# Weight splits through a PSUM copy, earlier keys for the second attention unit, and left output tiles finished ahead of right ones

## The chip, the core and the metric

The kernel runs on one core of a Trainium2 chip. A core has engines that each work through their own list of instructions in order: TensorE (PE in the profile, with PEld for its weight loads), VectorE (DVE), ScalarE (ACT), GpSimd (POOL), and SyncE (SP), whose list here holds DMA issues alone. They wait for each other through semaphores. An instruction that waits holds up all that stands behind it on the same engine. The metric is the device time of one execution in microseconds (us).

## What is computed

Two branches over the same input x of 2048 rows and 448 columns, mixed by a gate, all in float32:

```
g   = sigmoid((x * gate_w).sum(-1))
# A: 16 heads of 28, each row looks at 8 rows back at a stride of 2
q, k, v = split_heads(x @ wqkv)
idx     = pos[:, None] - 2 * arange(8)[None, :]
a       = softmax(where(idx >= 0, q . k[idx] / sqrt(28), -1e9)) . v[idx]   @ wo
# B: squared ReLU
b   = relu(x @ w1 + b1) ** 2 @ w2 + b2
out = g * a + (1 - g) * b
```

w1 is 448 x 1792, w2 is 1792 x 448, wo is 448 x 448.

## The kernel before

Every matmul operand is held as two parts: a rounded high part and the rest (low part). A product is three matmuls: high by high, high by low, low by high. A split is a copy on ACT that rounds (`split_full`, L115) and a subtraction on DVE that gives the rest (L116). K = 448 is three blocks of 128 and one of 64; two products of 64 rows are laid side by side on the upper and lower half of TensorE (`side_by_side`, L184), so one matmul pair takes the time of one. The halves swap after some pairs. Before a swap, a tiny write orders the new half behind the old: a memset on DVE into the accumulator (`turn`, L194), or a one-column ACT copy (`touch`, L516).

The rows are cut in four chunks of 512, each chunk in four tiles of 128 rows. There are two stages on TensorE.

**Stage A** makes q, k and v. Chunks 1 to 3 take two calls of `qkv_two` each, with 63 matmul pairs per call and six accumulators in PSUM banks of the two tags "m" and "b" (four banks each). ACT empties an accumulator into a staging tile (`qkv_evacuate`, L203, and L211 for the gate's column), SP stores it to DRAM (L209). The turns of a call stand after pairs 24, 33 and 42. Beside that, w1 (four pieces, `w1_piece`) and the first seven row blocks of w2 (two pieces, `w2_piece`) are loaded and split. All raw weights pass through a pool of two buffers, so a load waits until an earlier piece was read. In the last call the first MLP matmuls are laid between (`mlp_one` at pair 51, `mlp_two` at pair 57).

**Stage B** is the MLP, in the order of chunks 3, 0, 1, 2, with 7 steps per chunk. A step takes two blocks of 128 hidden columns: `h_first`, 12 matmul pairs; then `o_part(..., False)`, the first half of the output matmuls of the step before, for its left tiles (0, 1) and its right tiles (2, 3), 6 pairs each; `h_second`, 9 pairs; then `o_all(..., True)`, the second half of those output matmuls, 6 pairs left and 6 right. The result of h is squared on ACT (L565 to L567) and its low part made on DVE (L564), one for each of the two blocks; I call these two subtractions the first and the second h low. The next step's output matmuls need them. In the last step of a chunk the output accumulators are complete; `fin_add` (L751, DVE) scales them into a tile that SP stores. This falls in the first step of the next chunk, called the seam here. Its last lines before the change:

```
for tls in (left, right)[:1 if ends else 2]:
    o_part(pc, pf, False, tls)
o_turn(pc, pf, left if ends else both)
...
h_second(x, accs, f)
...
o_all(pc, pf, True)
```

**Attention** runs beside both stages, in 8 units (two halves of the rows by four groups of heads). POOL multiplies (L325 for q by k, L332 for weights by v), DVE sums (L326, L340), eight pieces per unit and product. POOL's products lie in four buffers, so POOL is at most four pieces ahead of DVE. After the fourth unit of a half, DVE transposes the sums in place (L342) and SP stores them; they come back for the matmuls with wo (`wo_first`, `wo_second`, tile "a").

**Who sets the order.** The kernel is recorded with a modelled TensorE clock: `advance(dt)` adds the estimated time of matmuls, and whatever is due by then is put on its engine's list: deferred work by `at(dt, ...)` and `when(t, ...)`, attention by the costs QK_COST, AV_COST, SM_COST and the waits ATT_DELAY (before the first unit) and KEY_DELAY (before the second). So constants in modelled nanoseconds decide where a subtraction stands between the sums on DVE, and where a load stands on SP. They decide no start times: these follow from the lists and the waits.

Of the kernel before, what the change touches and what calls it, by code (L numbers as in the profile page):

```python
# [14 lines left out]
P = 128  # L15
# [17 lines left out]
QK_COST = 2300.0  # L33
AV_COST = 2000.0
SM_COST = 600.0
ATT_DELAY = 20000.0
LO_DELAY = 1500.0
HL_DELAY = 1800.0
SPLIT_GAP = 2000.0
W2_GAP = 1500.0  # L40
ROW_GAP = 9200.0
OUT_DELAY = 2500.0
WO_DELAY = 4500.0
LOAD_DELAY = 1500.0
LAND_DELAY = 5000.0
OL_DELAY = 2500.0
KEY_DELAY = 10500.0
DEFER = 2
ORDER = (3, 0, 1, 2)
WARM = 13  # L50
# [7 lines left out]
def gated_mix_kernel(ctx: ExitStack, tc: tile.TileContext, xT, wqkv, w1, w2, wo, b1, b2, out):  # L58
# [169 lines left out]
    def accs(c, b, tls, tags):  # L228
        return [Acc(t, f"qkv{c}_{tl}_{b}", ncols(b)) for t, tl in zip(tags, tls)]

    def run(c, todo, steps):


        a = 0
        for e, done, *turns in steps:
            side_by_side(todo[0][a:e], todo[1][a:e])
            while a < e:
                advance(min(12, e - a) * MM448)
                a = min(a + 12, e)
# [30 lines left out]
            [(15, [], (v[0], v[1])), (24, [], (v[2], v[3])),  # L270
             (33, [(2, 0, v[0]), (2, 1, v[1])]), (42, [(2, 2, v[2]), (2, 3, v[3])])])

    def qkv_two(x, c, t0, beside=()):

        t1 = t0 + 1
        kinds = ("mm", "bm", "bb") if beside else ("mm", "mb", "bb")
        (q0, q1), (k0, k1), (v0, v1) = (accs(c, b, (t0, t1), tags) for b, tags in enumerate(kinds))
        run(c, [full(x, q0, t0, 0) + last(x, q0, t0, 0) + full(x, q1, t1, 0) + last(x, q1, t1, 0) + full(x, k0, t0, 1)
                + full(x, k1, t1, 1) + full(x, v0, t0, 2) + last(x, v0, t0, 2) + full(x, v1, t1, 2),
                full(x, k1, t1, 1) + last(x, k1, t1, 1) + full(x, v0, t0, 2) + full(x, v1, t1, 2) + last(x, v1, t1, 2)  # L280
                + full(x, q0, t0, 0) + full(x, q1, t1, 0) + full(x, k0, t0, 1) + last(x, k0, t0, 1)],
            [(24, [], (q0, k1)), (33, [], (q1, v0)), (42, [(0, t0, q0), (1, t1, k1)], (k0, v1)),
             (51, [(0, t1, q1)]), (51, [], *beside[:1]), (54, [(2, t0, v0)]), (57, [], *beside[1:]),
             (63, [(1, t0, k0), (2, t1, v1)])])
# [44 lines left out]
    def av_piece(u, par, g, v, lg, s):  # L329

        pr = prodp.tile([P, C, W], F32, tag="pp", name=f"av{u}_{s}", bufs=PP_BUFS)
        nc.gpsimd.tensor_mul(  # L332
            pr.rearrange("p (h d) w -> p w h d", h=HG),
            lg[:, s][:, :, :, None].to_broadcast([P, W, HG, DH]),
            v[:, s:s + W].rearrange("p w (h d) -> p w h d", h=HG),
        )
        o = o_t[par, s]

        def rest():
            nc.vector.tensor_reduce(o[:, g * C:(g + 1) * C], pr, axis=AX.X, op=ALU.add)  # L340
            if g == G - 1:
                nc.vector.transpose(o, o)  # L342
                at(OUT_DELAY, lambda: o_store(par, s))
        pending.append(rest)

    def o_store(par, s):
        nc.sync.dma_start(o_d[par, s], o_t.pop((par, s)))
        at(WO_DELAY, lambda: (wo_q.append((par, s)), wo_loads()))
# [102 lines left out]
    def at(dt, fn):  # L451

        later.append((clock["pe"] + dt, fn))
# [3 lines left out]

    def advance(dt):
        clock["pe"] += dt
        for item in sorted([x for x in later if x[0] <= clock["pe"]], key=lambda x: x[0]):  # L460
            later.remove(item)
            item[1]()
        if not clock["on"]:
            clock["att"] = clock["pe"]
            return
        while clock["att"] < clock["pe"]:
            try:
                r = next(att)
            except StopIteration:
                clock["on"] = False  # L470
                return
            if r is None:
                clock["att"] = clock["pe"]
                return
            clock["att"] += r
# [2 lines left out]
    def raw_tile(name):  # L478
        return rawp.tile([P, 4, 512], F32, tag="raw", name=name)

    def w1_piece(i, dt):

        n = F // 4
        raw = raw_tile(f"w1raw{i}")
        nc.sync.dma_start(raw[:, :, :n], w1[i])
        sl = slice(i * n, (i + 1) * n)

        def part(k):
            if k < 3:
                split_full(raw[:, k, :n], w1h[:, k, sl], w1l[:, k, sl], soon)  # L490
                return
            for a in range(i * n, i * n + n, 64):
                f, b = divmod(a, P)
                if b and a > i * n:
                    continue
                m = min(P - b, i * n + n - a)
                rows, o = slice(f % 2 * 64, f % 2 * 64 + 64), f // 2 * P + b
                split_full(raw[rows, 3, a - i * n:a - i * n + m], w17h[rows, o:o + m], w17l[rows, o:o + m], soon)
        for k in range(4):
            at(dt + k * SPLIT_GAP, lambda k=k: part(k))  # L500

    def w2_piece(i0, n, dt):
        raw = raw_tile(f"w2raw{i0}")
        nc.sync.dma_start(raw[:, :n, :D], w2[:, i0:i0 + n])
        for k in range(n):
            at(dt + k * W2_GAP, lambda k=k: split_full(raw[:, k, :D], w2ah[:, i0 + k], w2al[:, i0 + k], soon))

    def x_load(c):
        raw = raw_tile(f"xraw{c}")
# [138 lines left out]
            when(t + 4500.0, x_more, c + 1)  # L648
            when(t + 5000.0, lambda c: x_spill(c, xs[c]), c)
    when(10500.0, x_spill, 0, x)  # L650
    when(25000.0, w1_piece, 0, 13000.0)
    when(44500.0, halos)
    when(46500.0, w1_piece, 1, 12500.0)
    when(67000.0, w1_piece, 2, 10500.0)
    when(68000.0, w1_piece, 3, 15500.0)
    when(70000.0, biases)
    when(86000.0, w2_piece, 0, 4, 6500.0)
    when(91300.0, w2_piece, 4, 3, 6000.0)

    pair = {}  # L660

# [13 lines left out]
    for c in range(4):  # L675
        x = xs[c]
        if c == 0:
            qkv_first(x)
        else:
            qkv_two(x, c, 0)  # L680
            qkv_two(x, c, 2, (mlp_one, mlp_two) if c == 3 else ())
        if c == 1:
            st_["spilled"] = 0
            clock["on"] = True
            clock["att"] = clock["pe"] - 1.0
            advance(0.0)
        if c == 3:
            st_["spilled"] = 1
# [266 lines left out]
    for g in range(2, 2 * NF):  # L955
        i, f = g // (NF // 2), g % (NF // 2) * 2
        c = ORDER[i]
        pc, pf = (c, f - 2) if f else (ORDER[i - 1], NF - 2)
        ends = f == NF - 2 and i < 3
        last = g == 2 * NF - 1  # L960
        if not f:
            x, slots = X([nxt[j][0] for j in range(4)]), [nxt[j][1] for j in range(4)]
            nxt = {}
        accs = h_first(x, c, f)
        if f == 2 and 0 < i < 3:
            x_reload(i + 1, 3, free)
# [12 lines left out]
        if g == 2:  # L979
            o_all(c, 0, True)  # L980
            del hs[c, 0], hs[c, 1]
        for tls in (left, right)[:1 if ends else 2]:
            o_part(pc, pf, False, tls)
        o_turn(pc, pf, left if ends else both)
        if f in (NF - 6, NF - 4):
            for tl in left if f == NF - 6 else right:
                fin_prep(c // 2, (c % 2) * 4 + tl)
        h_second(x, accs, f)
        ops = mlp_ops(accs, c, f, (HL_DELAY, HL_DELAY if ends else 2 * HL_DELAY))
        emit(ops[:3])  # L990
# [12 lines left out]
        o_all(pc, pf, True)  # L1003
        del hs[pc, pf], hs[pc, pf + 1]
        if st:
            wo_second(st)
# [55 lines left out]
```

## Time and profile before

| | us |
|---|---|
| median of 3 runs | 423.88 |
| lowest and highest | 421.41, 424.59 |
| the profiled execution | 423.65 |
| its span, first to last instruction | 421.9 |
| TensorE busy in the span | 412.3 |
| POOL, DVE, ACT busy | 268.9, 260.9, 199.5 |

The profile is one execution; each time in it is counted from the start of its span. The time of an execution is 1.75 us longer than its span. A busy TensorE is not one at its peak, so idle time, and stretches in which fewer matmuls start, tell more than the share.

### The profile page before, as it was taken

How to read it: one execution, taken by the hardware profiler on the slowest of the kernel's cores; microseconds unless marked ns; L12 is line 12 of the kernel's file. 1: busy time of each engine (PE TensorE's matmuls, PEld its weight loads, DVE VectorE, ACT ScalarE, POOL GpSimd, SP SyncE). 2: the span in 40 equal slices, each digit the busy share in tenths (PEclk: the TensorE clock that was granted, in tenths of full speed). 3: DMA queues.
4: the chain of work that ended last, by engine and by line, in shares of the span. 5: the costliest groups of instructions: out<-in, count | busy, mean ns of one | idle time of the engine just before them, and what ended most of it. 6: DMA issues, size and time to landing. Idle time of an engine off the chain costs nothing.

```text
span 421.9 us, 9322 instructions
## 1 busy us (share of the span) xinstructions
PE 412.3 (98%) x3844; PEld 375.0 (89%) x3844; DVE 260.9 (62%) x403; ACT 199.5 (47%) x453; POOL 268.9 (64%) x167
## 2 busy tenths in 40 slices
PE   8999999999999999999999997999999999999995
PEld 8999999999799888888888886889998888888994
DVE  5420522384775776775776796798677577687343
ACT  4542555344566565445565342625552344346630
POOL 0000000950599999999898997799799879692000
PEclk9999999999999999999999998999999999999999
DMA  7999899938464053463220637882446320228804
GB/s 234 345 335 328 240 376 291 365 99 280 173 204 172 0 203 116 184 214 110 89 84 2 246 139 207 212 252 81 94 169 228 137 89 2 82 89 176 174 2 175
DMA packets 65322, 73.75 MB, mean 175 GB/s; under 512 B 32320, under 2 KB 58368, under 8 KB 64896
## 3 DMA queue, kind: packets, MB, share of 16 engines
q1 hardware_dynamic: 65280, 73.16, 52.9%
q8 instruction: 30, 0.49, 0.5%
q14 instruction: 12, 0.10, 0.1%
HBM read 45.71 MB, written 28.25 MB: 175 GB/s over the span
## 4 chain that ended last, share of the span: by engine, by line
PE 90%; DMA 3%; DVE 2%; POOL 2%; ACT 1%; SPq 0%; issue 0%; DVEq 0%; ACTq 0%
PE h L184 30%; PE b L184 29%; PE qkv L184 20%; PE a L184 8%; DMA w2raw<-w 3%; PE qkv L253 2%; POOL av L332 1%; DVE bt L751 1%; PE warm L576 1%; DVE o L340 1%; POOL w2bl L892 1%; DVE h L564 0%; SPq L710 0%; ACT st L203 0%; ACT w17h L115 0%
## 5 line engine op out<-in xcount | busy, mean ns | idle before, releaser
L325 POOL TENSOR_TENSOR qk<-q,k 128x896 f32<-128x896 f32 x64 | 135.9, 2156 | 104.2 <-DMA k<-k_d 89.3
L332 POOL TENSOR_TENSOR av<-lg,v 128x896 f32<-128x896 f32 x64 | 119.0, 1973 | 7.0 <-DMA v<-v_d 3.9
L184 PE MATMUL qkv<-wqh,x 64*128 64x448 f32 (+1 forms) x528 | 91.0, 362 | 0.0
L564 DVE TENSOR_TENSOR h<-h,h 128x512 fp32r<-128x512 f32 x56 | 38.6, 688 | 61.1 <-ACT h L567 60.8
L184 PE MATMUL qkv<-wql,x 64*128 64x448 f32 (+1 forms) x264 | 75.0, 362 | 0.0
L184 PEld LDWEIGHTS qkv<-wqh,x 64*128 64x128 f32 x528 | 74.0, 185 | 0.4
L184 PE MATMUL b<-w2ah,h 64*128 64x448 f32 x448 | 68.8, 364 | 2.5 <-DVE h L564 2.5
L326 DVE TENSOR_REDUCE lg<-qk 128x32 f32<-128x896 f32 x64 | 67.6, 1077 | 2.4 <-POOL qk L325 2.3
L340 DVE TENSOR_REDUCE o<-av 128x112 f32<-128x896 f32 x64 | 67.1, 1071 | 3.1 <-POOL av L332 2.9
L184 PE MATMUL b<-w2bh,h 64*128 64x448 f32 x448 | 66.6, 360 | 0.0
L565 ACT ACTIVATE h<-h,b1z 128x512 f32<-128x512 f32 x56 | 36.6, 654 | 41.0 <-PE h L184 41.0
L184 PEld LDWEIGHTS b<-w2ah,h 64*128 64x128 f32 x448 | 45.8, 186 | 6.8 <-DVE h L564 3.6
L184 PEld LDWEIGHTS b<-w2bh,h 64*128 64x128 f32 x448 | 41.9, 184 | 3.8 <-ACT h L516 0.3
L184 PEld LDWEIGHTS qkv<-wql,x 64*128 64x128 f32 x264 | 44.8, 185 | 0.2
L184 PE MATMUL b<-w2al,h 64*128 64x448 f32 x224 | 44.7, 362 | 0.0
L203 ACT ACTIVATE st<-qkv 128x448 f32<-128x448 f32 x48 | 24.6, 543 | 40.8 <-PE qkv L184 34.3
L184 PE MATMUL b<-w2bl,h 64*128 64x448 f32 x224 | 40.5, 359 | 0.0
L566 ACT ACTIVATE h<-h 128x512 fp32r<-128x512 f32 x56 | 33.5, 598 | 1.7
L567 ACT ACTIVATE h<-h 128x512 f32<-128x512 f32 x56 | 33.3, 594 | 0.0
L184 PE MATMUL h<-x,w1h 64*128 64x512 f32 x168 | 31.2, 387 | 0.0
L516 ACT ACTIVATE h<-h 128x4 fp32r<-128x4 f32 (+1 forms) x32 | 6.6, 207 | 47.0 <-PE b L184 46.9
L184 PE MATMUL h<-x1b,w1h 64*128 64x512 f32 x168 | 28.8, 395 | 0.0
(124 smaller groups left out, 718.0 us busy)
## 6 DMA issues: line engine op xcount, KB each, us to landing
k<-k_d SPq DMA_DIRECT2D x8, 840.0 KB, 5.3
v<-v_d SPq DMA_DIRECT2D x8, 840.0 KB, 4.7
x_d<-x SPq DMA_DIRECT2D x12, 512.0 KB, 5.2
q_d<-st SPq DMA_DIRECT2D x8, 448.0 KB, 6.5
k_d<-st SPq DMA_DIRECT2D x8, 448.0 KB, 5.6
v_d<-st SPq DMA_DIRECT2D x8, 448.0 KB, 7.4
w1raw<-w SPq DMA_DIRECT2D x4, 896.0 KB, 9.7
q<-q_d SPq DMA_DIRECT2D x8, 448.0 KB, 3.3
```

Source lines behind the costliest of these rows:

```text
L184: nc.tensor.matmul(acc.pt[:, :acc.n], a[rows], w[rows], start=acc.todo == acc.all, stop=acc.todo == 1)
L203: nc.scalar.activation(st[:, :, t % 2], pt[:, :D].rearrange("p (g c) -> p g c", g=G), AF.Copy)
L253: nc.tensor.matmul(acc.pt[:, :NQ], a, w, start=k == j == 0, stop=False)
L325: nc.gpsimd.tensor_mul(pr, q[:, s:s + 1].to_broadcast([P, W, C]), k[:, s:s + W])
L326: pending.append(lambda: nc.vector.tensor_reduce(lg[:, s], pr.rearrange("p w (h d) -> p w h d", h=HG), axis=AX.X, op=ALU.add))
L332: nc.gpsimd.tensor_mul(pr.rearrange("p (h d) w -> p w h d", h=HG), lg[:, s][:, :, :, None].to_broadcast([P, W, HG, DH]), v[:, s:s + W].rea ...
L340: nc.vector.tensor_reduce(o[:, g * C:(g + 1) * C], pr, axis=AX.X, op=ALU.add)
L516: nc.scalar.activation(ap, f32(ap), AF.Copy)
L564: nc.vector.tensor_sub(hl, pt, f32(hh))
L565: ops += [lambda pt=pt, r=r: nc.scalar.activation(pt, pt, AF.Relu, bias=b1t[:, f + r:f + r + 1]), lambda pt=pt, hh=hh: nc.scalar.activatio ...
L566: lambda pt=pt, hh=hh: nc.scalar.activation(hh, pt, AF.Square),
L567: lambda pt=pt, r=r, low=low: (nc.scalar.activation(pt, pt, AF.Square), at(delays[r], low))]
```

## The change

It has five parts.

1. The pieces 2 and 3 of w1 and both pieces of w2 are split by `split_copied`: ACT writes the high part as before and then a second, plain copy of the raw block into a PSUM bank (`copy_tile`, one of the four banks "b" in each of the last two calls of `qkv_two`); DVE subtracts the high part from that copy. Only ACT now reads the raw block. There is one bank, so a copy waits until the subtraction before has read it. Each piece gets an absolute modelled time and its own gap in place of SPLIT_GAP and W2_GAP; the second piece of w2 is loaded earlier.
2. ATT_DELAY falls from 20000 to 17000, KEY_DELAY from 10500 to 6000: all of attention stands earlier on the lists, and the keys of the second unit are loaded ahead of the stores of the last chunk's first tiles.
3. In the seam step the left tiles' second half is moved up, between the first half and `h_second`; the right tiles' stays behind. The touch is made for left and right apart.
4. The eight transposes of the first half of the rows are spread, each 2000 modelled ns behind the one before.
5. The second h low becomes due 3200 modelled ns after its step where it was 3600; items that fall due together are taken again in order of time (`advance`).

```diff
-ATT_DELAY = 20000.0
+ATT_DELAY = 17000.0
-SPLIT_GAP = 2000.0
-W2_GAP = 1500.0
+COPY_DELAY = 1300.0
+OUT_GAP = 2000.0
-KEY_DELAY = 10500.0
+KEY_DELAY = 6000.0
...
+        if copies:
+            copy_tile()
...
-            if g == G - 1:
+
+            def out():
                 nc.vector.transpose(o, o)
                 at(OUT_DELAY, lambda: o_store(par, s))
+            if g == G - 1 and par:
+                out()
+            elif g == G - 1:
+
+                at(s * OUT_GAP, out)
...
+    copy = [None, 0]
+
+    def copy_tile():
+
+
+        assert not copy[1]
+        copy[0] = ps("b", f"copy{len(later)}")
+
+    def split_copied(t, raw, parts):
+
+        assert not copy[1]
+        pt = copy[0]
+        n = raw.shape[-1]
+        for rows, cols, hi, _ in parts:
+            nc.scalar.activation(hi, raw[rows, cols], AF.Copy)
+        nc.scalar.activation(pt[:, :n], raw, AF.Copy)
+        copy[1] += 1
+
+        def lows():
+            for rows, cols, hi, lo in parts:
+                nc.vector.tensor_sub(lo, pt[rows, cols], f32(hi))
+            copy[1] -= 1
+        when(t + COPY_DELAY, lows)
...
+            if k < 3 and i > 1:
+                split_copied(dt + k * gap, raw[:, k, :n], [(slice(0, P), slice(0, n), w1h[:, k, sl], w1l[:, k, sl])])
+                return
...
-    when(25000.0, w1_piece, 0, 13000.0)
+    when(25000.0, w1_piece, 0, 38000.0, 2000.0)
-    when(46500.0, w1_piece, 1, 12500.0)
-    when(67000.0, w1_piece, 2, 10500.0)
-    when(68000.0, w1_piece, 3, 15500.0)
+    when(46500.0, w1_piece, 1, 58500.0, 1500.0)
+    when(67000.0, w1_piece, 2, 77400.0, 1450.0)
+    when(68000.0, w1_piece, 3, 83300.0, 1450.0)
-    when(86000.0, w2_piece, 0, 4, 6500.0)
-    when(91300.0, w2_piece, 4, 3, 6000.0)
+    when(86000.0, w2_piece, 0, 4, 93000.0, 1400.0)
+    when(89600.0, w2_piece, 4, 3, 100200.0, 1400.0)
...
-            qkv_two(x, c, 0)
-            qkv_two(x, c, 2, (mlp_one, mlp_two) if c == 3 else ())
+            qkv_two(x, c, 0, copies=c == 3)
+            qkv_two(x, c, 2, (mlp_one, mlp_two) if c == 3 else (), c == 3)
...
+        done = pf == NF - 2
         for tls in (left, right)[:1 if ends else 2]:
             o_part(pc, pf, False, tls)
-        o_turn(pc, pf, left if ends else both)
+            if done:
+                o_turn(pc, pf, tls)
+        if done:
+
+            o_part(pc, pf, True, left)
+        else:
+            o_turn(pc, pf, left if ends else both)
...
-        ops = mlp_ops(accs, c, f, (HL_DELAY, HL_DELAY if ends else 2 * HL_DELAY))
+        ops = mlp_ops(accs, c, f, (HL_DELAY, HL_DELAY if ends else 3200.0))
...
-        o_all(pc, pf, True)
+        for tls in (left, right)[1 if done else 0:]:
+            o_part(pc, pf, True, tls)
```

The number of matmuls, sums and loads stays the same; ACT gets 15 copies more. On TensorE the order changes at the three seams only.

More of the change, by code (lines that the diff above doesn't have):

```diff
@@ L271, in qkv_first, with qkv_two @@
              (33, [(2, 0, v[0]), (2, 1, v[1])]), (42, [(2, 2, v[2]), (2, 3, v[3])])])
-    def qkv_two(x, c, t0, beside=()):
+    def qkv_two(x, c, t0, beside=(), copies=False):
         t1 = t0 + 1
@@ L459, in advance @@
         clock["pe"] += dt
-        for item in sorted([x for x in later if x[0] <= clock["pe"]], key=lambda x: x[0]):
+        while due := [x for x in later if x[0] <= clock["pe"]]:
+            item = min(due, key=lambda x: x[0])
             later.remove(item)
@@ L479, in raw_tile, with w1_piece @@
         return rawp.tile([P, 4, 512], F32, tag="raw", name=name)
-    def w1_piece(i, dt):
+    copy = [None, 0]
[15 more added lines that the diff above has]
+        when(t + COPY_DELAY, lows)
+    def w1_piece(i, dt, gap):
         n = F // 4
@@ L491, in part @@
                 return
+            parts = []
             for a in range(i * n, i * n + n, 64):
@@ L497, in part, with w2_piece @@
                 rows, o = slice(f % 2 * 64, f % 2 * 64 + 64), f // 2 * P + b
-                split_full(raw[rows, 3, a - i * n:a - i * n + m], w17h[rows, o:o + m], w17l[rows, o:o + m], soon)
+                parts.append((rows, slice(a - i * n, a - i * n + m), w17h[rows, o:o + m], w17l[rows, o:o + m]))
+            if i > 1:
+                split_copied(dt + k * gap, raw[:, 3, :n], parts)
+                return
+            for rows, cols, hi, lo in parts:
+                split_full(raw[rows, 3, cols], hi, lo, soon)
         for k in range(4):
-            at(dt + k * SPLIT_GAP, lambda k=k: part(k))
-    def w2_piece(i0, n, dt):
+            when(dt + k * gap, part, k)
+    def w2_piece(i0, n, t, gap):
         raw = raw_tile(f"w2raw{i0}")
@@ L505, in w2_piece @@
         for k in range(n):
-            at(dt + k * W2_GAP, lambda k=k: split_full(raw[:, k, :D], w2ah[:, i0 + k], w2al[:, i0 + k], soon))
+            when(t + k * gap, lambda k: split_copied(t + k * gap, raw[:, k, :D], [
+                (slice(0, P), slice(0, D), w2ah[:, i0 + k], w2al[:, i0 + k])]), k)
     def x_load(c):
```

## The prediction

> **What bounds the kernel now.** I read the page's busy shares first, then TensorE's waits, then the windows and the timeline around each wait. The fences hold picked rows, not stretches.
>
> ```profile
> span 421.9 us, 9322 instructions
> PE 412.3 (98%) x3844; PEld 375.0 (89%) x3844; DVE 260.9 (62%) x403; ACT 199.5 (47%) x453; POOL 268.9 (64%) x167
> PE b L184 <- DVE h L564: 2.5, 2, 2.1
> ```
>
> TensorE is busy 98% of the span and no matmul is added or removed, so all that can be won is what TensorE loses today. Past the start-up its waits are two on a subtraction of h (L564; 2.5 us in total, the longest 2.1) and one of 1 us on an evacuation, below. In the windows around the longest:
>
> ```profile
> 253.60:255.80 2.20, 0.07 (x2) 0.00 (x0) 2.20 (x5) 0.00 (x0) 2.20 (x2) 1.00 0.17 65
> 256.50:259.80 3.30, 3.30 (x20) 2.72 (x19) 3.23 (x5) 0.21 (x1) 2.12 (x2) 0.50 1.02 338
> ```
>
> The columns are PE, PEld, DVE, ACT and POOL busy, then the granted clock, DMA share and rate. TensorE stands for 2.2 us, and just after that its clock is 0.50 for 3.3 us, in which half the work is lost: 1.65 us. This seam (chunk 0 to chunk 1) costs 2.2 + 1.65 = **3.85 us**. The two others:
>
> ```profile
> 98.58 0.37 SPq L504 DMA_DIRECT2D w2raw<-w  x1
> 106.62 0.58 ACT L115 ACTIVATE w2ah<-w2raw 128x448 fp32r<-128x448 f32 x1 [4.22 <-DMA w2raw<-w]
> 107.53 0.16 ACT L211 ACTIVATE zg<-qkv 128x1 f32<-128x1 f32 x1
> 107.74 0.49 PE L184 MATMUL h<-x,w17h 64*128 64x512 f32 x1 [0.97 <-ACT zg L211]
> ```
>
> w2's second piece is issued at 98.58 and lands 8 us later. Its split stands on ACT ahead of an evacuation, and the first h matmul needs the bank which that evacuation frees: **1.0 us**. The third:
>
> ```profile
> 136.72 1.09 DVE L340 TENSOR_REDUCE o<-av 128x112 f32<-128x896 f32 x1 [0.68 <-POOL av L332]
> 137.76 0.36 PE L184 MATMUL b<-w2al,h 64*128 64x448 f32 x1
> 138.46 0.67 PE L184 MATMUL b<-w2ah,h 64*128 64x448 f32 x4 [0.35 <-DVE h L564]
> ```
>
> From 137.76 to 138.46 TensorE starts nothing where the next start is due after 0.2: **0.5 us**. An attention sum on DVE waits for POOL, and the h low stands behind it. The sum of what can be won is 3.85 + 1.0 + 0.5 = 5.35 us, and nothing else on TensorE's list stands still between start-up and end.
>
> **Part 1, the splits.** They lie in the last two calls of stage A.
>
> ```profile
> 84.06 1.98 ACT L115 ACTIVATE w1h<-w1raw 128x448 fp32r<-128x448 f32 x4
> 85.65 0.14 DVE L194 MEMSET qkv<- 1x1 f32 x2 [4.96 <-PE qkv L184]
> 89.92 0.06 DVE L194 MEMSET qkv<- 1x1 f32 x2
> 91.83 0.54 ACT L203 ACTIVATE st<-qkv 128x448 f32<-128x448 f32 x1 [5.80 <-PE qkv L184]
> L116 DVE TENSOR_TENSOR w1l<-w1raw,w1h x12: 610/626/2586, 47.4 to 96.0; 128x448 fp32r<-128x448 f32 x12
> L885 ACT ACTIVATE c<-w2raw x5: 529/531/534, 128.1 to 167.1; 128x448 f32<-128x448 f32 x5
> L886 DVE TENSOR_TENSOR w2bl<-c,w2bh x5: 573/624/627, 129.6 to 167.7; 128x448 fp32r<-128x448 f32 x5
> L326 DVE TENSOR_REDUCE lg<-qk 128x32 f32<-128x896 f32 x64 | 67.6, 1077 | 2.4 <-POOL qk L325 2.3
> ```
>
> The kernel already splits other rows this way: copy 0.53, subtraction from the copy 0.62, against 0.63 median and 2.59 worst from the raw block. Fifteen copies add 15 x 0.53 = 8 us to ACT between 84 and 111; ACT is busy for 47% of the span, so the room is there. That alone costs TensorE nothing, and DVE is spared the 2.6 us case.
>
> What can cost is DVE's order. In the changed list the chain after 84.06 is: high, copy and low of the first block (done 85.7), a sum (86.8), the second low (87.4), the third, whose copy had to wait for the bank until 87.4 (88.6), a sum (89.65), the first turn, the four narrow lows of w17 (about 1.2 together, 91.0), a sum (92.05), and only then the **second turn**. Before, it ran at 89.92. The evacuation at 91.83 starts when pair 42 is done, and the pair behind it needs the second turn: about 91.6. So TensorE waits 92.1 - 91.6 = 0.5 us. The bounds are 0 (if copies and lows overlap better) and 1.1 (one more sum). I take 0.5, the chain as it stands. The first turn (89.7 against 89.8 needed) and the third just fit; so does the evacuation of the call's second q, which the next call's first pair needs (about 95.9 against 96.4).
>
> The 1.0 us wait goes: w2's second piece now stands on ACT behind the q and k evacuations of the last call. Its load is still issued near 100, behind three stores on SP, so it lands near 106, or at 108 if it takes 8 us again, and is first needed near 107.7; what is late next is the touch behind it, with 0.8 us to spare. Net of stage A: 1.0 - 0.5 = **0.5 us won**.
>
> **Part 2, attention earlier.**
>
> ```profile
> 90.00 2.50 POOL L325 TENSOR_TENSOR qk<-q,k 128x896 f32<-128x896 f32 x1 [2.10 <-DVE qkv L194]
> 99.05 1.41 SPq L301 DMA_DIRECT2D q<-q_d  x1
> 109.90 6.69 POOL L325 TENSOR_TENSOR qk<-q,k 128x896 f32<-128x896 f32 x3 [17.40 <-DMA k<-k_d]
> 128.21 2.28 POOL L892 TENSOR_TENSOR w2bl<-w2raw,w2bh 128x448 fp32r<-128x448 f32 x2
> ```
>
> POOL stood 17.4 us for the second unit's keys. Their load needs only the buffer that POOL leaves at 92.5, but was issued behind three stores (q from 99.05). Now it stands ahead of these and goes out about 92; POOL starts near 98.5, 11 us earlier. About 3 us of that go back: two subtractions of w2 (L892) now stand behind the third product of the first unit, which POOL reaches near 123, while their rows come near 126 (they ran at 128.2, with POOL late itself). POOL is not on TensorE's path, so this is worth nothing by itself. It does take away the wait at 137: the sums ahead of that h low are done by about 136, the second low at 137.1, just in time. **0.5 won**, bounds 0 and 0.5.
>
> The keys' load also passes two later places on SP. The x tiles of the next chunk stood ahead of the sixth unit's keys and now stand behind them and behind the first stored sum:
>
> ```profile
> 231.55 4.92 SPq L717 DMA_DIRECT2D x1b<-x_d  x3
> ```
>
> SP held there until 236.5, because the x slots came free. POOL, some 8 us earlier, leaves the keys' buffer near 229 and the first transpose is done near 233.3, so both are through before the slots are free: nothing.
>
> **Parts 3 to 5, the seams.** Call H the end of `h_second`. First a common step, then the seam before the change (the chain for PE, the timeline for DVE).
>
> ```profile
> 197.72 2.04 PE h L184 x18
> 199.76 2.40 PE b L184 x24
> 202.16 2.72 PE h L184 x24
> 201.61 0.69 DVE L564 TENSOR_TENSOR h<-h,h 128x512 fp32r<-128x512 f32 x1 [3.50 <-ACT h L567]
> 203.30 0.69 DVE L564 TENSOR_TENSOR h<-h,h 128x512 fp32r<-128x512 f32 x1
> ```
>
> ```profile
> 245.52 2.04 PE h L184 x18
> 247.56 1.22 PE b L184 x12
> 248.80 1.28 DVE L751 SCALAR_TENSOR_TENSOR bt<-b,zg,bt 128x448 f32<-128x448 f32 x2 [0.53 <-PE b L184]
> 249.99 0.68 DVE L564 TENSOR_TENSOR h<-h,h 128x512 fp32r<-128x512 f32 x1
> 250.59 1.08 DVE L340 TENSOR_REDUCE o<-av 128x112 f32<-128x896 f32 x1
> 251.70 0.65 DVE L342 STREAM_TRANSPOSE o<-o 128x448 f32<-128x448 f32 x1
> ...
> 253.92 1.24 DVE L751 SCALAR_TENSOR_TENSOR bt<-b,zg,bt 128x448 f32<-128x448 f32 x2
> 255.07 0.68 DVE L564 TENSOR_TENSOR h<-h,h 128x512 fp32r<-128x512 f32 x1
> ```
>
> In the common step H is 199.76; ACT lets the lows start at H + 1.85 and H + 3.54, so the second is done at H + 4.2. Needed is the first at the third pair of the next output matmuls and the second at the sixth: H + 2.4 + 2.72 + 0.4 = H + 5.5, and H + 6.1. At the seam H is 247.56, and two sums, two transposes and both scalings stand ahead of the second low, which is done at H + 8.2: 2.1 late.
>
> After the change the left tiles are complete before `h_second`, so two of four scalings run early. But only 1.2 us of output matmuls follow H instead of 2.4, so the lows are needed at H + 4.3 and **H + 4.9**. DVE's new order at this seam: right scalings (from H + 1.25, 1.24: H + 2.5), one transpose (H + 3.15), first low (H + 3.8), a sum (H + 4.9), second low (H + 5.5). It is 0.6 late. At chunk 3 to 0 both lows follow the scalings directly (ACT ends last, H + 4.2); at chunk 1 to 2 a sum lies between without a transpose (H + 4.9 to 5.0, 0.1 late). So the seams pay 0.7 in place of 3.85: **3.15 won**. Bounds for the 0.6: nothing, if the second low's place is reached with the sum done early, and 1.7, one more sum.
>
> A stall of 0.6 should leave the clock alone: behind the 0.97 wait at 107.74 matmuls ran at full rate, behind 2.2 us they did not. The Trainium skill ("TensorE: Matmul & The Clock Gate", Part 1) says that the array falls to half its clock after an idle window of about 3.4 us. By that rule 2.2 us would not be enough, the half clock would have another cause, and its 1.65 us would stay. The trace, with 0.50 right behind a 2.2 us stand, speaks against it.
>
> **The sum.** Stage A 0.5, the wait at 137 0.5, the seams 3.15: 4.15 us off the profiled execution's 423.65 gives 419.5. That execution is 0.2 below the median of 423.88, so 419.5 is 1.0% below the median, just where a measurement of this kernel can tell a difference from none (1%, 4.2 us).
>
> **Rivals.**
>
> *The half clock stays, or a seam still idles near 2 us.* For it: the second low has only 0.7 us between its natural end (H + 4.2) and its need. Against: the new order has one sum and one transpose ahead of it where there were two of each. Time: 419.5 + 1.65 = 421.2, with a longer wait 422.5.
>
> *Stage A collides.* One copy bank ties ACT's evacuations to DVE's sums; the margins above are 0.1 to 0.8 us. If two of them fail by a sum each, 2 x 1.1 is lost: 421.7. Against: DVE is rid of its 2.6 us subtractions there.
>
> *Slower: the tighter seams.* All three need the lows 1.2 us earlier. If a sum in front of the second low waits for POOL, the low slips at more than one seam; from 2.2 us late on the clock falls too and each costs 3.85, as the one seam does now. Two such seams give 423.65 - 1.0 + 3.85 = 426.5, three 430.3. Against: POOL is some 8 us earlier and the lists only 7.5 modelled us, so its products should lie ready.
>
> **How the numbers follow.** The forecast (418.3, all 5.35 won, to 420.8) has 0.60, the first rival 0.16, the second 0.12, the slower one 0.12. The range for 8 in 10 runs from 417.8, half a microsecond under the best case, to 422.9, past the first two rivals. Faster by over 1% means under 419.6: three quarters of the forecast and little else, 0.47. Slower by over 1% is the third rival, 0.12; the rest, 0.41, lies within 1%.
>
> **What would show it.** TensorE's waits: no 1.0 on the evacuation, a new one near 0.5 on a memset (L194) around 92, and on L564 a largest wait of 0.6 near 252 in place of 2.1. The clock at 1.00 all through. POOL's first wait on k as before, the 17.4 us one near 6. The forecast is wrong if TensorE stands over 2 us anywhere, if a window shows 0.50, or if x1b or an evacuation appears among its waits.

## The result and the profile after

The changed kernel takes 420.48 us (median of 20 runs, 419.78 to 422.68) against 423.09 for the kernel before (20 runs): a ratio of 0.9943, 95% interval 0.9925 to 0.9962. That is 0.6% faster, clear of the noise but under the 1% from which the prediction counts a change, and 1 us above the 419.5 forecast. The gain is 2.6 us where 4.15 was forecast. The profiled execution took 421.8. One execution further on, the profiled one of the splits alone, took 428.5 us where the ten others of its kernel took 421.1 to 423.8, and nothing is read from its waits.

The page of the kernel after, its span and busy line, and then TensorE's waits from its view of waits (engine, line, waited-for instruction: us in total, times, longest):

```profile
span 419.9 us, 9331 instructions
PE 411.9 (98%) x3844; PEld 376.3 (90%) x3844; DVE 255.7 (61%) x403; ACT 207.8 (49%) x471; POOL 268.6 (64%) x167
```

```profile
PE h L184 <- DMA x2b<-x_d: 1.7, 2, 1.5
PE warm L619 <- DVE zero L617: 1.2, 1, 1.2
PE b L184 <- DVE h L607: 0.4, 1, 0.4
```

The 2.1 us wait on a low of h and the 1.0 us on an evacuation are gone. In their place stands one at a seam that the prediction did not look at: TensorE waits for x tiles of chunk 2 at the seam from chunk 1 to chunk 2. The timeline of the kernel after, picked matmuls of TensorE: the first h matmuls of stage A and the stands at the two seams:

```profile
106.28 0.56 PE L184 MATMUL h<-x,w17h 64*128 64x512 f32 x2
...
251.97 0.47 PE L184 MATMUL b<-w2ah,h 64*128 64x448 f32 x2 [0.37 <-DVE h L607]
...
323.68 0.39 PE L184 MATMUL h<-x2b,w1h 64*128 64x512 f32 x2
325.53 0.50 PE L184 MATMUL h<-x2b,w1h 64*128 64x512 f32 x2 [1.46 <-DMA x2b<-x_d]
...
326.10 0.39 PE L184 MATMUL h<-x2b,w1h 64*128 64x512 f32 x2
326.74 0.50 PE L184 MATMUL h<-x2b,w1h 64*128 64x512 f32 x2 [0.25 <-DMA x2b<-x_d]
```

A next start is due after 0.2 us, so the stand ahead of 325.53 is 1.85 - 0.2 = 1.65 us; the one ahead of 326.74 is 0.64 - 0.2, or 0.4. The matmul at 251.97 is the one that started at 255.80 before: 3.83 us had been won by then. The windows of the kernel after (us, then PE, PEld, DVE, ACT and POOL busy, the granted clock, DMA share, GB/s):

```profile
323.70:325.50 1.80, 0.37 (x4) 0.00 (x0) 1.80 (x3) 0.00 (x0) 1.80 (x2) 1.00 0.92 378
327.40:330.70 3.30, 3.30 (x21) 2.88 (x19) 0.00 (x0) 0.41 (x2) 3.30 (x2) 0.50 0.02 5
```

The clock of 0.50 now stands behind this stand: 3.3 us of it lose 1.65 us. So this seam costs 1.65 + 0.4 + 1.65 = **3.7 us** in the profiled execution. It doesn't do so in every execution. Those 3.3 us lower the mean granted clock of a run to about 0.996; 7 of the 20 runs show 0.996 or less and take 421.5 to 422.7, the other 13 take 419.8 to 420.8.

Why the tiles are late is on SP. First the timeline of SP before the change, then after it (start, duration of the issue):

```profile
320.33 0.40 SPq L717 DMA_DIRECT2D x2b<-x_d  x1
320.82 1.83 SPq L731 DMA_DIRECT2D bt<-f_d  x4
323.21 1.00 SPq L717 DMA_DIRECT2D x2b<-x_d  x2
325.87 0.32 SPq L307 DMA_DIRECT2D v<-v_d  x1
```

```profile
315.39 0.41 SPq L760 DMA_DIRECT2D x2b<-x_d  x1
315.88 1.84 SPq L774 DMA_DIRECT2D bt<-f_d  x4
317.82 0.38 SPq L309 DMA_DIRECT2D v<-v_d  x1
318.25 0.91 SPq L760 DMA_DIRECT2D x2b<-x_d  x2
```

With attention earlier, the sixth unit's v tile (128 x 1680 numbers of 4 bytes, 840 KB) has passed the last two x tiles. The view of the x2b tile at this place, kernel after, gives the time from issue to landing; its median for the same three tiles was 4.9 us before:

```profile
DMA to landing us min/median/max: 4.1/7.2/8.0
```

### The profile page after: what moved, and what is told of

It reads as the page before. It is cut to its first block, busy times and chain, and to the rows that moved or that the text cites. A ratio compares the mean times of both kernels' runs of the same rounds, so it can differ in the third digit from the quotient of the medians.

```text
span 419.9 us, 9331 instructions
## 1 busy us (share of the span) xinstructions
PE 411.9 (98%) x3844; PEld 376.3 (90%) x3844; DVE 255.7 (61%) x403; ACT 207.8 (49%) x471; POOL 268.6 (64%) x167
## 4 chain that ended last, share of the span: by engine, by line
PE 94%; DVE 2%; DMA 2%; ACT 1%; issue 0%; DVEq 0%
PE h L184 31%; PE b L184 31%; PE qkv L184 21%; PE a L184 8%; PE qkv L253 2%; DMA x2b<-x_d 2%; DVE lg L328 1%; PE warm L619 1%; DVE bt L794 0%; DVE w1l L510 0%; DVE h L607 0%; ACT copy L505 0%; ACT st L203 0%; DVE w17l L510 0%; DVEq L1108 0%
## 5 line engine op out<-in xcount | busy, mean ns | idle before, releaser
L184 PEld LDWEIGHTS qkv<-wqh,x 64*128 64x128 f32 x528 | 71.7, 184 | 1.2 <-DVE qkv L194 0.5
L184 PE MATMUL qkv<-wql,x 64*128 64x448 f32 (+1 forms) x264 | 71.2, 361 | 0.0
L184 PE MATMUL b<-w2bh,h 64*128 64x448 f32 x448 | 69.4, 365 | 0.0
L184 PEld LDWEIGHTS b<-w2ah,h 64*128 64x128 f32 x448 | 48.1, 184 | 3.8 <-DVE h L607 0.9
L184 PEld LDWEIGHTS b<-w2bh,h 64*128 64x128 f32 x448 | 47.0, 188 | 3.6 <-ACT h L559 0.3
L184 PE MATMUL b<-w2al,h 64*128 64x448 f32 x224 | 46.3, 359 | 0.0
L184 PE MATMUL b<-w2bl,h 64*128 64x448 f32 x224 | 45.0, 364 | 0.0
L184 PEld LDWEIGHTS qkv<-wql,x 64*128 64x128 f32 x264 | 42.5, 184 | 0.2
L184 PE MATMUL h<-x,w1h 64*128 64x512 f32 x168 | 33.9, 386 | 0.0
L184 PE MATMUL h<-x2b,w1h 64*128 64x512 f32 x168 | 29.0, 392 | 1.7 <-DMA x2b<-x_d 1.7
```

Of the source, the lines that this page charges most:

```text
L184: nc.tensor.matmul(acc.pt[:, :acc.n], a[rows], w[rows], start=acc.todo == acc.all, stop=acc.todo == 1)
```

## The experiments

The theory after the first look: the v tile, brought forward by part 2, delays the x tiles, and parts 3 to 5 win at the seam from chunk 0 to 1 what was worked out. The rivals: the x tiles are late for another reason; the half clock comes by itself; and part 2, not parts 3 to 5, clears the seam. The letters A, B and C name the theories as each expectation has them. TensorE's wait of 1.2 us on `zero` at the start-up is in every kernel and is mostly left out below. Every run stands beside runs of the kernel before on the same chip (medians 423.4 to 423.9).

**The v tile behind the x tiles.**

```diff
+        held[0] = ends
         accs = h_first(x, c, f)
...
             x_reload(i + 1, 2, slots[0])
             free = slots[1]
+            held[0] = False
+            free_loads()
```

where `free_loads` issues the attention loads that are due, unless they are held.

> The changed kernel with one move on SP: the attention loads (q, k, v) that fall due while the second h matmuls of a chunk's last step are built are held back until the next chunk's x tiles have been issued. In the instruction lists this moves a single transfer, the sixth unit's v tile (840 KB), from ahead of the last two x2b tiles of the seam from chunk 1 to chunk 2 to behind them; PE, DVE, ACT and POOL keep their order. Theory A (the v transfer ahead of them makes the x tiles land late): TensorE's waits on x2b (1.65 and 0.4 us near 324) go, the two tiles land in about 5 us instead of 7.2, no window shows a clock of 0.50, and the time is the changed kernel's 420.5 less 2.0 us less the half clock it has in some executions: 418.2 to 418.5. Rival B (the x tiles are late because their slots come free late, at 318, whatever is in the queue): the waits stay near 2 us and so does the time, 420.2 to 421.8. Rival C (the half clock is not tied to a stand of TensorE but comes by itself): the waits go, but a window of 0.50 still shows in some executions and the times still lie in two groups 1.7 us apart.

Measured: 418.39 us (418.0 to 418.69), ratio 0.9886 (0.9855 to 0.9918). SP's timeline, the landing of the x2b tiles and TensorE's waits in this kernel:

```profile
317.64 0.96 SPq L764 DMA_DIRECT2D x2b<-x_d  x2
318.65 0.42 SPq L309 DMA_DIRECT2D v<-v_d  x1
```

```profile
DMA to landing us min/median/max: 4.4/5.6/6.3
```

```profile
PE warm L623 <- DVE zero L621: 1.2, 1, 1.2
PE b L184 <- DVE h L611: 0.4, 1, 0.4
```

One transfer moved, and the wait on x2b is gone: the two tiles are issued right behind the four loads and the median tile lands 1.6 us faster. No run of six shows a mean clock under 0.997. Theory A holds, B and C fall: the two sets of times, 419.8 to 420.8 and 421.5 to 422.7, have become one.

**Half of the v tile ahead.**

```diff
...
+        if held[0]:
+            m = 7
+            nc.sync.dma_start(v[:, :m], src[:, :m * C])
+            late.append(lambda: nc.sync.dma_start(v[:, m:], src[:, m * C:]))
...
```

> The changed kernel with the sixth unit's v tile loaded in two pieces: the first 7 of 15 rows (392 KB) where the whole tile (840 KB) stood, ahead of the last two x2b tiles, the other 8 behind them. With 840 KB ahead those tiles landed 7.2 us and 8.0 us after their issue and TensorE stood 1.65 and 0.4 us; with nothing ahead (v held) 5.6 and 6.3 us and it stood 0.3 at most. Theory A (the bytes ahead in the queue make the delay): about half the delay, landings near 6.4 and 7.1 us, stands of 0.8 and 0.3 us in sum 0.7 to 1.4, no clock of 0.50, 419.0 to 419.6. Rival B (a transfer ahead costs by its being there, not by its bytes): stands as in the changed kernel, 420.2 or more. Rival C (only a whole tile matters): no stand, 418.4.

Measured: 419.04 us (418.92 to 419.47), ratio 0.9884 (0.9845 to 0.9923). TensorE's wait on the tiles in this kernel, and their landing:

```profile
PE h L184 <- DMA x2b<-x_d: 0.9, 2, 0.6
```

```profile
DMA to landing us min/median/max: 4.7/6.4/7.2
```

With 0, 392 and 840 KB of v ahead of them the median x tile lands after 5.6, 6.4 and 7.2 us in these three profiles, and the times follow: 418.4, 419.0, 420.5. That is the order theory A expects, and neither B nor C. That the delay goes by the bytes, 0.8 us for each half, is less sure than it looks: each landing is from one execution, and a run below with nothing of v ahead has 6.1. The Trainium skill ("DMA: Bandwidth & Descriptors", section "Two DMAs through the same engine are not ordered") says that descriptors in one queue of one DMA engine start in order; the three landings agree.

**Parts 1 and 2 alone** (the seams as before: no left tiles first, no spread transposes, the old delay of the h low).

```diff
-            if g == G - 1 and par:
+            if g == G - 1:
                 out()
-            elif g == G - 1:
-
-                at(s * OUT_GAP, out)
...
-        done = pf == NF - 2
+        done = False
...
-        ops = mlp_ops(accs, c, f, (HL_DELAY, HL_DELAY if ends else 3200.0))
+        ops = mlp_ops(accs, c, f, (HL_DELAY, HL_DELAY if ends else 2 * HL_DELAY))
```

> The changed kernel with the seams as before (parts 3 to 5 undone): only the copied splits of stage A and the earlier attention are left. By the prediction's sum this is worth 0.5 + 0.5 = 1.0 us of 423.1, so 422.1; the long stand of 2.2 us near 254 and the clock of 0.50 behind it stay. Theory A (the sixth unit's v load, which the earlier attention sends ahead of the x2b tiles, makes them late): a wait on x2b at the seam from chunk 1 to 2 shows here too, though smaller, since without part 3 the second tile is needed 1.2 us later: 0 to 1 us, and the time is 422 to 423. Rival B (that wait belongs to part 3): none on x2b, 422.1 or less.

Measured: **417.50 us** (417.39 to 417.71), ratio 0.9866 (0.9828 to 0.9905), 3 us better than the change as a whole (ratio 0.9943). Theory A had expected 422 to 423; B's "none on x2b, 422.1 or less" holds by its words, but neither saw a gain of this size, and B's reason, part 3, falls with the run without part 3 below. TensorE's wait on a low, and DVE at the seam from chunk 0 to 1:

```profile
PE b L184 <- DVE h L604: 0.2, 1, 0.2
```

```profile
247.74 0.65 DVE L345 STREAM_TRANSPOSE o<-o 128x448 f32<-128x448 f32 x1
248.31 1.23 DVE L791 SCALAR_TENSOR_TENSOR bt<-b,zg,bt 128x448 f32<-128x448 f32 x2
249.46 0.68 DVE L604 TENSOR_TENSOR h<-h,h 128x512 fp32r<-128x512 f32 x1
250.06 1.27 DVE L791 SCALAR_TENSOR_TENSOR bt<-b,zg,bt 128x448 f32<-128x448 f32 x2
251.24 0.68 DVE L604 TENSOR_TENSOR h<-h,h 128x512 fp32r<-128x512 f32 x1
```

The code at the seam is that of the kernel before, but no sum and no transpose stands between the lows any more: the fourth unit's last pieces are through by 248.4. They had lain in the seam because attention was late, and part 2 alone takes them out. The x tiles aren't late either, although v is ahead of them here too: it goes out at 314.29, 3.5 us ahead of the last two, and the four loads of stored output tiles don't lie between; the median tile lands after 4.2 us.

**The earlier attention alone**, on the kernel before.

```diff
-ATT_DELAY = 20000.0
+ATT_DELAY = 17000.0
-KEY_DELAY = 10500.0
+KEY_DELAY = 6000.0
```

> The kernel before with part 2 alone: the two delays that bring the attention forward (17000 and 6000), nothing else. Theory A (it was POOL's lateness that laid two sums and two transposes into the seam from chunk 0 to 1, and the earlier attention alone clears it): the 2.2 us stand near 254 and the clock of 0.50 behind it go, no more than 0.5 us is left there, the wait of 0.5 us at 137 goes too, and the 1.0 us on an evacuation at 107 stays or changes by some tenths, since the splits of w2's second piece are as before: 423.4 - 3.6 - 0.5 = 419.3, so 418.8 to 420. Rival B (the prediction's view: the seam's order is what must change): the stand near 254 stays at 1.5 us or more, and the time is 422 or more.

Measured: 425.06 us (423.5 to 428.74), ratio 1.0034 (1.0005 to 1.0063). The seam behaves as theory A says, and the time still misses it by 6 us. TensorE's waits, the timeline of SP and ACT around w2's second piece, and two windows:

```profile
PE h L184 <- ACT zg L211: 4.5, 1, 4.5
PE qkv L184 <- DVE qkv L194: 0.7, 1, 0.7
PE b L184 <- DVE h L564: 0.2, 1, 0.2
```

```profile
95.99 1.23 SPq L301 DMA_DIRECT2D q<-q_d  x1
97.27 0.42 SPq L302 DMA_DIRECT2D k<-k_d  x1
...
99.38 4.20 SPq L504 DMA_DIRECT2D w2raw<-w  x1
...
110.81 0.58 ACT L115 ACTIVATE w2ah<-w2raw 128x448 fp32r<-128x448 f32 x1 [8.90 <-DMA w2raw<-w]
```

```profile
110.42:113.83 3.41, 1.90 (x10) 1.53 (x12) 2.41 (x3) 3.02 (x9) 3.41 (x3) 0.50 0.02 5
113.83:117.25 3.42, 3.42 (x20) 2.72 (x18) 3.42 (x3) 0.37 (x1) 3.42 (x2) 0.50 0.41 134
```

The wait on the h low is down to 0.2, the 2.2 us stand near 254 is gone. But the second unit's loads now go out just ahead of w2's second piece, whose split lands on ACT ahead of an evacuation: 4.5 us of TensorE, with 6.8 us of half clock from 110.4 on, and 0.7 us more on a turn. It looks like what happened to the x tiles, at another place: a bulk load moved ahead of one that TensorE needs; no run moves this load alone. In the changed kernel, with part 1, the first piece of w2 is out at 89 and the keys at 92, well ahead of the second piece at 98.6.

**The splits alone** (parts 2 to 5 undone).

```diff
-ATT_DELAY = 17000.0
+ATT_DELAY = 20000.0
-KEY_DELAY = 6000.0
+KEY_DELAY = 10500.0
```

on the kernel with parts 1 and 2.

> The kernel with part 1 alone: the copied splits of w1 and w2 and their load times, with both attention delays as before (20000 and 10500) and the seams as before. The prediction gives the splits the 1.0 us evacuation wait at 107 and charges them the second turn near 91. Theory A: no wait at 107, 0 to 0.3 us near 91, the 2.2 us stand near 254 with its clock of 0.50 and the 0.5 at 137 as before: 423.4 - 0.8 = 422.6, so 422 to 423.4. Rival B (the splits by themselves also bring POOL forward, since DVE is rid of the 2.6 us subtractions): the stand near 254 shrinks to under 1.5 us and the time is below 421.

Measured: 422.92 us (421.08 to 428.46), ratio 0.9965 (0.9938 to 0.9993): as theory A expected. The order at the seam is that of the kernel before, and 5 of the ten runs up to 423.8 us show a mean clock of 0.996 or less.

**Parts 3 to 5 alone**, on the kernel before.

```diff
+        done = pf == NF - 2
...
+                at(s * 2000.0, out)
...
-        ops = mlp_ops(accs, c, f, (HL_DELAY, HL_DELAY if ends else 2 * HL_DELAY))
+        ops = mlp_ops(accs, c, f, (HL_DELAY, HL_DELAY if ends else 3200.0))
```

with the seam's order as in the change.

> The kernel before with parts 3 to 5 alone (left output tiles finished ahead of the second h matmuls, transposes spread, the h low's delay 3200, the planner's loop): the splits of stage A and the keys' load as before. The prediction's sum gives the seams 3.15 us, of which 0.6 is paid back at the seam from chunk 0 to 1. Here POOL is late as before, so the sixth unit's v load stays behind the x2b tiles. Theory A (the seams give what was worked out, and only the earlier attention brings the x2b wait): 423.1 less 3.2 to 3.8, so 419.3 to 419.9, the waits of 1.0 us at 107 and 0.5 us at 137 still there, no wait on x2b, no clock of 0.50. Rival B (the x2b wait comes from the seam's shorter run, which needs the x tile 1.2 us earlier): TensorE waits on x2b here too, 1 us or more, and the time is 421 or more.

Measured: 420.76 us (419.25 to 422.75), ratio 0.9941 (0.9915 to 0.9967), between the two theories. Its waits:

```profile
PE b L184 <- DVE h L570: 1.1, 2, 0.8
PE h L184 <- ACT zg L211: 1.1, 1, 1.1
PE h L184 <- DMA x0b<-x_d: 0.6, 2, 0.4
```

The 2.2 us stand is gone here too (0.3 is left of it), so parts 3 to 5 and part 2 each clear the same seam, and together they can't win it twice. The wait at 107 stays; the one at 137 is 0.8 in place of 0.4. No x2b wait, as theory A said; the one on x0b, at the seam from chunk 3 to 0, was expected by nobody. There the list of SP is that of the kernel before, with the loads of q and k directly ahead of the x tiles. But k landed 7.8 us after its issue where it took 5.0 before, and the median x0b tile 7.4 where it took 5.0: in this execution the same transfers were slower, and why isn't known. A margin of 2 us at a seam can thus be lost with no change of the list.

**Part 3 undone, part 4 undone.** Each on the changed kernel, the first with the edit `done = False`, the second with the transposes at once again.

> The changed kernel with part 3 alone undone: each chunk's left output tiles are finished behind the second h matmuls, as before; splits, attention, spread transposes and the h low's delay stay changed. On DVE the first transpose of the three is gone from the seam and the second low stands behind two scalings, one low, two scalings and a transpose; it is needed 1.2 us later than with part 3 (H + 6.1 in place of H + 4.9). Theory A (it was the transposes and the sum in front of the second low that made the 2.2 us, and they are gone without part 3): the seam from chunk 0 to 1 stands 0 to 0.7 us, the x2b wait is shorter than in the changed kernel by up to 1.2 us, the time is 418.5 to 420. Rival B (part 3 is what removed the stand, since the second low is ready about H + 7): a stand of 1 us or more near 252, and the time is 420.5 or more.

> The changed kernel with part 4 alone undone: the transposes of a first-half unit's sums follow their sums at once, as before; left tiles first, splits, attention and the h low's delay stay changed. Of the kernels run so far, the two with the x2b wait (the changed one and the one without part 3) have part 4 and the earlier attention together; their SP list has the four loads of stored output tiles at the end of chunk 1, ahead of the sixth unit's v tile. With part 4 undone the attention outputs are stored earlier, the output projection takes its turns a step earlier, and the list has two of the four loads at 292 and two at 306, as in the kernel with the seams as before, where v was issued at 314.3 instead of 317.8 and TensorE did not wait. Theory A (the x2b wait needs part 4 together with part 2): no wait on x2b, v issued near 314, no clock of 0.50, 417.5 to 418.5. Rival B (part 3, with its earlier need, is enough): a wait on x2b of 0.5 us or more, 419 or more.

Measured: 420.16 us (419.49 to 423.06; 0.9929, 0.9899 to 0.9960) without part 3, 418.76 (418.5 to 420.26; 0.9892, 0.9859 to 0.9925) without part 4; theory A's ranges end 0.2 and 0.3 us lower. The waits of each, in this order:

```profile
PE h L184 <- DMA x2b<-x_d: 1.7, 2, 1.5
```

```profile
PE b L184 <- DVE h L604: 0.9, 2, 0.7
```

The x2b wait is the same without part 3, to the tenth; that it would shrink by up to 1.2 us was wrong. Without part 4 it is gone: v goes out at 315.23 and the last two x tiles at 318.73. So it takes part 2 and part 4 together (with part 1 in each of these kernels). Spread transposes store the attention results later, the projection with wo takes its turns about 9 us later (f_d is stored at 300.15 and 314.38, against 291.53 and 305.29 without part 4), and SP stands until then with the x tile, four loads and v behind it. What the kernel without part 4 pays instead is the low at the seam from chunk 0 to 1, 0.9 us: there, four scalings, a low and a sum stand ahead of the second low, and part 3 needs it 1.2 us sooner.

**v held and part 3 undone.**

> The changed kernel with part 3 undone and the v tile held behind the x2b tiles: the run with v held (418.4) and this one differ in part 3 alone, and the run with part 3 undone (420.2, with a wait of 1.5 + 0.3 us on x2b) and this one in the v tile's place alone. Theory A (part 3 is no gain once the attention is early, since it needs the lows 1.2 us sooner): no wait of 0.3 us or more on a low at the seam from chunk 0 to 1 where the kernel with part 3 stands 0.5, none on x2b, no clock of 0.50; 417.2 to 417.9, at or under the run with v held. Rival B (part 3 pays): a stand of 0.5 us or more on a low at a seam, and 418.9 or more.

Measured: 418.16 us (417.3 to 419.07), ratio 0.9860 (0.9825 to 0.9896). TensorE's wait on the tiles, and their landing:

```profile
PE h L184 <- DMA x2b<-x_d: 0.3, 1, 0.3
```

```profile
DMA to landing us min/median/max: 5.0/6.1/6.7
```

The low's wait is gone, as A expected. Two things miss A: a wait of 0.3 us on x2b is left, with nothing of v ahead of these tiles, and the time is above A's range. There is no stand of 0.5 us on a low, and the ranges of this kernel and of the one with v held (418.0 to 418.7) overlap: B falls too. With attention early and the transposes spread, part 3 neither wins nor loses a measurable amount.

**A version meant to be better still**: parts 1 and 2 with other delays.

```diff
-ATT_DELAY = 17000.0
+ATT_DELAY = 18500.0
-KEY_DELAY = 6000.0
+KEY_DELAY = 4500.0
```

> A version meant to beat both: the splits and the earlier attention with the seams as before (the kernel that took 417.5), and the delays 18500 and 4500 in place of 17000 and 6000, which only puts the fifth sum of the first unit behind the second evacuation turn of the call instead of ahead of it, and the keys' load ahead of one more store. Expected: the 0.3 us wait of TensorE near 91 goes and nothing else moves: 417.2 (417.0 to 417.5). If a sum or split that now stands later is missed in its place, a new wait of about 1 us shows between 91 and 108 and the time is 418 or more.

Measured: 419.44 us (418.63 to 420.92), ratio 0.9903 (0.9870 to 0.9937): a miss. The expectation has the keys' place the wrong way round: they stand behind one more store, not ahead of it. SP issues them at 96.78 in place of 91.76, and on DVE the second unit's sums wait for POOL with the lows of w2 behind them:

```profile
109.49 1.09 DVE L328 TENSOR_REDUCE lg<-qk 128x32 f32<-128x896 f32 x1 [1.01 <-POOL qk L327]
110.49 0.61 DVE L507 TENSOR_TENSOR w2al<-copy,w2ah 128x448 fp32r<-128x448 f32 x1
```

ACT can't write the only copy bank until that low has read it, a touch stands behind, and TensorE waits 1.8 us at 110. In the profiled execution a clock of 0.50 follows:

```profile
112.52:115.93 3.41, 3.41 (x20) 2.67 (x18) 2.61 (x3) 1.61 (x4) 3.41 (x3) 0.50 0.01 2
```

The 0.3 us at 91 is won as meant, and six times as much is lost. The lowest time of the kernels run is thus that of parts 1 and 2 alone. By the ratio to the kernel before on the same chip (0.9866) it isn't told apart from v held with part 3 undone (0.9860).

## Why the prediction was right or wrong, point by point

- **The time.** 419.5 was forecast, 420.5 measured, inside the range. The larger chance, 0.47, was on faster by over 1%; it came out within 1%, which had 0.41. That the time is so near is partly luck, for errors nearly cancel: more was won than the sum says, and a cost was left out. The kernel with v held has neither x wait nor half clock and takes 418.4, 1.1 under the forecast. And the base moved: the median before was 423.88 in three runs and 423.09 in twenty.
- **Stage A: 0.5 won forecast, about 1.1 measured; the mechanism right, the size off.** The evacuation wait is gone: the h matmul that started at 107.74 before is the second of the two at 106.28, 1.3 us sooner, of which 0.2 had been there by 89. By the starts that wait had cost 1.2 and not 1.0 (106.38 to 107.74 where 0.2 was due). The new wait on the second turn, priced at 0.5, is 0.3. DVE's order came as worked out; the second turn ran at 91.4 in place of 92.05.
- **The wait at 137.** Gone, as forecast. The output matmul that started at 138.46 before starts at 136.36, 2.1 sooner, so about 0.8 came here in place of 0.5.
- **The seam from chunk 0 to 1.** The second low was to be 0.6 late: the start at 251.97 comes 0.73 - 0.2 = 0.53 after it was due. The clock stays at 1.00 behind it, as forecast. Right in size. But the 1.65 us of half clock in the sum was its price in one execution. Its mark, a mean clock of 0.996 or less, is on 35 of 58 runs of the kernel before, so on average it cost about 1.0 us (an estimate: 35/58 of 1.65). What failed besides is the credit. The prediction gave parts 3 to 5 the 3.15 us and part 2 only 0.5. Part 2 alone clears the seam (a longest wait of 0.2) with its code unchanged. The prediction compared the order before with the list of the whole change, in which attention is earlier too, and credited all of the difference to parts 3 to 5.
- **The step that failed: the queues that part 2 is moved past.** The prediction followed the keys' load past two places on SP and the x1b tiles, and concluded "nothing". The seam from chunk 1 to 2 was not looked at. There v passes the last two x2b tiles, and that costs 2.05 us, and 1.65 more in the runs with half clock. The first rival's half clock came, but at another seam and behind a DMA, not behind a low.
- **The rivals.** Stage A did not collide; the kernel with other delays shows how little is missing: keys issued 5 us later, with the attention's start delayed too, cost 1.8 us. The slower rival did not come, as its premise (sums waiting for POOL at the seams) didn't: in the profile after, three sums on DVE wait for POOL (at 140, 149 and 360 us), none of them at a seam.
- **The signs named.** Of those that would show the forecast wrong, "if a window shows 0.50" came true, and "if x1b or an evacuation appears among its waits" nearly: it was x2b. No stand is over 2 us. Of the signs for it, the 1.0 us on the evacuation is gone, the low near 252 is 0.5 late, and POOL's wait on k fell from 17.4 to 6.3 us where "near 6" was named.

## What to carry to other kernels

When work is brought forward, list each transfer that it issues and what that now precedes on its queue, at every place and not at the first only; a bulk load ahead of a tile that is needed soon delays that tile (here 840 KB, by 1.1 to 1.6 us). Before crediting two edits with the same stall, run each alone: here each cleared it, and the pair of smaller edits was better than all five. A delay that looks harmless on one engine (spread transposes) can put off the stores and loads that hang on it by some nine microseconds.

## What the runs showed of the hardware

The half clock doesn't come in every execution, and it comes more often behind longer stands. Five kernels have no stand of 1 us behind the start-up in their profile (v held, half of it held, parts 1 and 2, part 4 undone, v held with part 3 undone): none of their 26 runs has a mean clock under 0.997. At 0.996 or less were 11 of 30 runs behind 1.65 + 0.4 us (the changed kernel and the one without part 3), 35 of 58 behind 2.2 us (the kernel before), 12 of 12 behind 4.5 us (attention alone). Two counts fit less plainly: parts 1 and 2 with other delays had 1 of 6 behind 1.8 us; and parts 3 to 5 alone, with 1.1 us at most in its profile, had 2 of 12, and what those two runs waited for isn't known.

The traces also show what decides between the two. In every profile the granted clock changes, between the start-up and the end, only at whole multiples of 3.413 us from one change to the next; in the kernel before, the stretches are 249.17, 3.41 and 160.43 us, that is 73, 1 and 47 of them. Here are the windows of that grid in the changed kernel, then in the kernel without part 3, whose profiled execution has the same two waits on x2b and no half clock behind them:

```profile
323.92:327.34 3.42, 1.71 (x14) 0.99 (x14) 2.50 (x3) 0.00 (x0) 3.42 (x3) 1.00 0.45 183
327.34:330.75 3.41, 3.41 (x22) 2.99 (x20) 0.00 (x0) 0.41 (x2) 3.41 (x2) 0.50 0.02 5
```

```profile
321.17:324.58 3.41, 2.50 (x24) 1.85 (x20) 3.31 (x5) 1.12 (x3) 3.41 (x3) 1.00 0.98 396
324.58:328.00 3.42, 2.59 (x22) 1.94 (x24) 1.44 (x2) 0.21 (x1) 3.42 (x2) 1.00 0.28 113
328.00:331.41 3.41, 3.41 (x35) 2.97 (x32) 0.00 (x0) 0.21 (x1) 2.79 (x2) 1.00 0.00 0
```

In the first both stands fall into one window, in which TensorE is idle for 1.7 us of 3.4, and the next window has the clock of 0.50. In the second the edge of a window falls into the first stand, so that one window has 0.9 us idle and the next 0.8, and the clock stays at 1.00. The other profiles agree: behind a window with 2.1 us idle (the kernel before), 1.8 (the other delays) and 3.0 (attention alone) the clock is 0.50; behind 1.0 (the kernel before, at 107) and 0.9 (half of v held) it is 1.00. Between 1.0 and 1.7 us no window at full clock was seen, so where the limit lies there stays open. The edges lie at other times in each execution, which would explain why the same stand is followed by either clock.

So the prediction was too sure in taking 1.65 us as the price of every execution. The Trainium skill ("TensorE: Matmul & The Clock Gate", Part 1) describes an activity window of 3413 ns that runs freely; the spacing above agrees. Its idle window of about 3.4 us as the condition does not fit, since 1.7 us of idle time in one window were enough.
